# Decode attention: one head's keys for all four batches in one DMA of 16 KB runs, with the scores reading them by stride

## Chip, cores, metric

The kernel runs on one core of one Trainium2 chip. The metric is the device time of one execution in microseconds. "Fast" is the undisturbed state of the chip.

## The reference, cut to what matters

```python
# x: (4 batches, 1 token, D=512). Attention A and gated unit B, applied twice: A B A B
W = 2048                                   # last W keys of a cache of 8192
q = (layernorm(x) @ wq)                    # 32 query heads of 128, 8 key heads, 4 query heads per key head
k = k_cache[:, :, Sk - W:, :]              # (4, 8, 2048, 128) bf16, the same in both attention layers
scores = einsum(q, k) * 128 ** -0.5
x = x + softmax(scores) @ v @ wo           # then x = x + GLU(layernorm(x))
```

For one token per batch there is little arithmetic and much to read: K is 16.8 MB, V as much per layer, weights the rest.

## The kernel before

One Python program makes a list of operations, a list scheduler orders them for each engine with a table of estimated durations, and semaphores are assigned. SBUF holds an arena of 49 slots; a slot is 128 partitions x 4 KB and takes one 512 KB transfer. Loads are issued in one fixed order from the sync queue, and a load waits until its slot is free. K stays in SBUF from layer one to layer two (32 slots); V is loaded twice, except for two tiles that are kept.

A unit of work is one key head with its four batches:

```python
def kv_d(cache, b, h):                       # 512 KB: partition p holds keys 16p..16p+15, a run of 4 KB
    return cache[b, h, SK - W:SK, :].rearrange("(p j) d -> p (j d)", p=128)

# layer one only: transpose K in place on VectorE, 32x32 blocks of 4-byte words (two bf16 each)
v32 = slot_ap(s).bitcast(F32)
P.op("vector", "T%d_%d" % (h, b), ..., lambda v, v32=v32: v.transpose(v32, v32), ...)

# scores: 4 chunks of the contraction x 4 batches; the four batches go to four column groups of PE
for cp in range(4):
    for gi, (h, b) in enumerate(pairs):
        kt = slot_ap(ks[gi]).rearrange("p (j c k t) -> p c t j k", c=2, k=32, t=2)
        pe.matmul(ps[32 * gi:32 * gi + NR, bank, :], qbd[:, q0:q0 + NR],
                  kt[:, cp // 2, cp % 2, :, :], start=(cp == 0), stop=(cp == 3))
```

`t` is the half of a 4-byte word, so neighbouring columns of the moving operand `kt` lie 4 bytes apart. After the scores come maximum, exponential, a matmul and a transpose that turn P (`pt`), the PV matmuls (64 per unit, 16 for each V tile), and the wo matmuls. The order on PE is: scores of unit u+2, then PV of unit u.

Of the kernel before, what the change touches and what calls it, by code (L numbers as in the profile page):

```python
# [6 lines left out]
F32 = mybir.dt.float32  # L7
# [239 lines left out]
class _SlotPool:  # L247
# [13 lines left out]
_TM = dict(  # L261
    sem_lat=100.0, pick_tol=60.0,
    dma_issue=60.0, dma_lat0=900.0, dma_lat1=1100.0, dma_max_out=16,
    bw_4k=412.0, bw_3k=409.0, bw_1k=356.0,
    pe_pair=38.0, pe_small=230.0, pe_f32=450.0, pe_row=80.0, pe_sq=300.0,
    dve_fix=150.0, dve_f32=1.04, dve_small=90.0,
    act_fix=180.0, act_el=0.833,
# [3 lines left out]
def build(nc, A_x, A_k, A_v, A_wq, A_wo, B_wg, B_wu, B_wd, out, cfg=None):  # L271
# [20 lines left out]
    SLOT = NJ * 128  # L292
# [19 lines left out]
    with es:  # L312
# [35 lines left out]

        P = _Plan()
        pool = _SlotPool(NS)  # L350
        SB = (0, 1)
        PB = 2
        OBS = (3, 4)
# [23 lines left out]
        loads = []  # L377
        where = {}

        def take_load():  # L380
            name, emit = loads.pop(0)
            s = pool.alloc()
            where[name] = s
            emit(s)

        def fill():
            while loads and pool.free:
                take_load()

        def need(name):  # L390
            while name not in where:
# [2 lines left out]

        def done(name):
            pool.release(where.pop(name))

        def load_kv(name, cache, b, h):
            loads.append((name, lambda s: dma(str(name), slot_ap(s), kv_d(cache, b, h), w=[("slot", s)])))
# [222 lines left out]
            return [[(h, b) for h in range(u * nh, (u + 1) * nh) for b in g] for u in range(HKV // nh)]  # L622

        def k_transpose(pairs):
            for (h, b) in pairs:
                s = need(("K", h, b))
                v32 = slot_ap(s).bitcast(F32)
                P.op("vector", "T%d_%d" % (h, b), c_dve(1024), lambda v, v32=v32: v.transpose(v32, v32),  # L628
                     r=[("slot", s)], w=[("slot", s)])

        ucount = [0]

        def softmax_unit(tag, pairs):
            u = ucount[0]
            ucount[0] += 1
            k2 = u % 2
            bank = SB[k2]
            ob = OBS[k2]
            ks = [where[("K", h, b)] for (h, b) in pairs]

            def e_s(pe):
                last = None
                for cp in range(4):
                    for gi, (h, b) in enumerate(pairs):
                        kt = slot_ap(ks[gi]).rearrange("p (j c k t) -> p c t j k", c=2, k=32, t=2)
                        q0 = ((b * HKV + h) * 4 + cp) * NR
                        last = pe.matmul(ps[32 * gi:32 * gi + NR, bank, :], qbd[:, q0:q0 + NR],  # L647
                                         kt[:, cp // 2, cp % 2, :, :], start=(cp == 0), stop=(cp == 3))
                return last
            P.op("tensor", "S" + tag, 16 * tm["pe_row"], e_s,  # L650
                 r=[("slot", s) for s in ks] + [("q", i, a) for i in set(h // 4 for (h, b) in pairs) for a in range(4)],
                 w=[("pss", k2)], banks=(bank,))
            mk = mxt[:, k2 * 32:(k2 + 1) * 32]
            P.op("vector", "mx" + tag, c_dve(512),
                 lambda v: v.tensor_reduce(nmax[:, k2:k2 + 1], ps[:, bank, :], AXX, ALU.max),  # L655
                 r=[("pss", k2)], w=[("mx", k2)], banks=(bank,))
            P.op("vector", "mk" + tag, tm["dve_small"],
                 lambda v: v.tensor_scalar(mk, maskr[:, :], nmax[:, k2:k2 + 1], None, ALU.add),
                 r=[("mx", k2), ("maskr",)], w=[("mk", k2)])
            P.op("vector", "nm" + tag, tm["dve_small"],  # L660
                 lambda v: v.tensor_reduce(nmax[:, 2 + k2:3 + k2], mk, AXX, ALU.max, negate=True, apply_transpose=True),  # L661
                 r=[("mk", k2)], w=[("nm", k2)])
            P.op("scalar", "ex" + tag, c_act(512) + 200.0,
                 lambda a: a.activation(prow[:, :], ps[:, bank, :], ACTF.Exp, bias=nmax[:, 2 + k2:3 + k2], scale=1.0,  # L664
                                        accum_out=psm[:, k2:k2 + 1]),
                 r=[("pss", k2)] + [("nm", k2)], w=[("prow",), ("psm", k2)], banks=(bank,))
            return k2

        def turn_p(tag, k2):
            ob = OBS[k2]  # L670
            P.op("tensor", "pp" + tag, tm["pe_sq"],
                 lambda pe: pe.matmul(ps[:, PB, :], perm[:, :], prow[:, :], start=True, stop=True),  # L672
                 r=[("prow",), ("perm",)], w=[("ppb",)], banks=(PB,))
            P.op("vector", "pt" + tag, c_dve(512),
                 lambda v: v.transpose(ebuf[:, k2 * 512:(k2 + 1) * 512], ps[:, PB, :]),  # L675
                 r=[("ppb",)], w=[("e", k2)], banks=(PB,))
            hi, mid, lo = (s3[:, k2 * 3 + n:k2 * 3 + n + 1] for n in range(3))
            sp, sr = psm[:, k2:k2 + 1], sres[:, k2:k2 + 1]
            P.op("gpsimd", "s1" + tag, 200.0, lambda g: g.tensor_copy(hi, sp), r=[("psm", k2)], w=[("s3", k2, 0)])  # L679
            P.op("gpsimd", "s2" + tag, 200.0, lambda g: g.tensor_tensor(sr, sp, hi, ALU.subtract),  # L680
                 r=[("psm", k2), ("s3", k2, 0)], w=[("sr", k2)])
            P.op("gpsimd", "s3" + tag, 200.0, lambda g: g.tensor_copy(mid, sr), r=[("sr", k2)], w=[("s3", k2, 1)])
            P.op("gpsimd", "s4" + tag, 200.0, lambda g: g.tensor_tensor(lo, sr, mid, ALU.subtract),
                 r=[("sr", k2), ("s3", k2, 1)], w=[("s3", k2, 2)])

            def e_sb(pe):
                last = None
                for n, sn in enumerate((hi, mid, lo)):
                    last = pe.matmul(ps[:, ob, 128:128 + NR], sn.broadcast_to([128, 128]), sel_b[:, :],  # L689
                                     start=(n == 0), stop=(n == 2))  # L690
                return last
            P.op("tensor", "sb" + tag, 3 * tm["pe_pair"], e_sb,
                 r=[("s3", k2, n) for n in range(3)] + [("sel_b",)], w=[("psb", k2)], banks=(ob,))
            rv = rinv[:, k2 * NR:(k2 + 1) * NR]
            P.op("vector", "ri" + tag, c_dve(NR) + 60.0,
                 lambda v: v.reciprocal(rv, ps[:, ob, 128:128 + NR]),
                 r=[("psb", k2)], w=[("rinv", k2)], banks=(ob,))
# [50 lines left out]
        def attn(L, gi_, wb):  # L748
            g = GROUPS[gi_]
            us = units_of(g)  # L750
            if L == 2:
                us = us[::-1]
            kuse = 2 * gi_ + (0 if L == 0 else 1)

            def front(ui):
                if L == 0:
                    k_transpose(us[ui])
                k2 = softmax_unit("%d.%d.%d" % (L, gi_, ui), us[ui])
                if L == 2:
                    for p in us[ui]:  # L760
                        done(("K",) + p)
                    fill()
                return k2

            ks = {}
            for ui in range(2):
                ks[ui] = front(ui)
                turn_p("%d.%d.%d" % (L, gi_, ui), ks[ui])
            for ui, pairs in enumerate(us):
                tag = "%d.%d.%d" % (L, gi_, ui)  # L770
                if ui + 2 < len(us):
                    ks[ui + 2] = front(ui + 2)
                ov = pv_unit(tag, pairs, ks[ui], keep if L == 0 else ())
                if ui + 2 < len(us):
                    turn_p("%d.%d.%d" % (L, gi_, ui + 2), ks[ui + 2])
                wo_unit(tag, kuse, wb, pairs, ov, ks[ui], ui == 0, ui == len(us) - 1)
            nb = len(g)
            P.op("vector", "xa%d_%d" % (L, gi_), tm["dve_fix"] + 40.0,
                 lambda v: v.tensor_tensor(bview(xT[:, 0:NX], g[0], g[-1] + 1),
                                           ps[:, wb, 0:NC * nb].rearrange("p (c b) -> p c b", b=nb),  # L780
                                           bview(xT[:, 0:NX], g[0], g[-1] + 1), ALU.add),
                 r=[("psw", wb)] + [("xT", b) for b in g], w=[("xT", b) for b in g], banks=(wb,))
# [66 lines left out]
        add_weights("wq", 0)  # L849
        for gi, g in enumerate(GROUPS):  # L850
            us = units_of(g)
            for (h, b) in us[0] + us[1]:
                load_kv(("K", h, b), A_k, b, h)
            for ui, pairs in enumerate(us):
                if ui + 2 < len(us):
                    for (h, b) in us[ui + 2]:
                        load_kv(("K", h, b), A_k, b, h)
                hs = set(h for h, b in pairs)
                add_weights("wo", 2 * gi, [("wo", h) for h in hs])
                for (h, b) in pairs:  # L860
                    load_kv(("V", h, b), A_v, b, h)
# [104 lines left out]
```

## Time and profile before

| | |
|---|---|
| time, median | 193.9 us |
| span of the profiled run | 191.3 us |
| bytes read | 72.9 MB |
| PE / VectorE busy | 53% / 46% |

In the profiles PE is TensorE (the matmuls), DVE is VectorE, ACT is ScalarE; `L647` is line 647 of the kernel. These are lines of the page of the kernel before: the span, the busy tenths in 40 slices of PE and DMA, the granted PE clock in tenths, and what the DMA engines moved in each slice of 4.8 us.

```profile
span 191.3 us, 4412 instructions
PE   0443224564617264171654436454885999985643
PEclk9999999999999999999999999999995555555555
DMA  4999999999999999999999999999999999999990
GB/s 123 342 413 412 409 409 389 410 393 404 408 392 411 388 406 410 390 411 392 398 398 388 406 407 359 388 380 413 409 409 405 411 406 407 407 407 406 403 366 17
```

The DMA row is full from the third slice to the last but one, near 410 GB/s. The dips to about 390 recur once per unit (about every 11.7 us), as the wo transfers (runs of 1 KB) do, and the dip around slice 25 is the first GLU, where loads wait for slots. So the kernel runs at the pace of the stream. But PE is at 9 tenths in slices 32 to 35: in layer two there is not much room behind the stream.

These are one layer-two unit on PE and the last matmuls that wait for the stream, from the timeline of the kernel before (start, duration, engine and line, how many; in brackets the idle time before and what ended it). A 0.25 us group (L689) is left out.

```profile
153.74 1.88 PE L647 MATMUL ps<-arena,qbd 128*16 128x512 bf16 x16
155.65 0.57 PE L739 MATMUL ps<-onb,arena 128*128 128x4 bf16 x16
156.08 1.85 PE L709 MATMUL ps<-ebuf,arena 128*128 128x4 bf16 x64
157.82 0.61 PE L672 MATMUL ps<-prow,perm 128*128 128x512 bf16 x1
158.36 1.88 PE L647 MATMUL ps<-arena,qbd 128*16 128x512 bf16 x16
...
187.07 1.01 PE L831 MATMUL ps<-hT,arena 128*128 128x4 bf16 x24 [0.63 <-DMA arena<-in_B_w_down_dram]
```

A unit's scores (L647) come 4.62 us apart (158.36 - 153.74). The four V tiles of a unit take 4 x 1.28 = 5.1 us to arrive. So PE has 0.5 us of room per unit. The last w_down lands at 187.07 us, and only 4.2 us of span come after it.

These two lines are the groups of the K transposes and of the score matmuls (busy us, mean ns of one, idle before).

```profile
L628 DVE STREAM_TRANSPOSE arena<-arena 128x1024 f32<-128x1024 f32 x32 | 38.2, 1217 | 0.7 <-DMA arena<-in_A_k_cache_dram 0.3
L647 PE MATMUL ps<-arena,qbd 128*16 128x512 bf16 x256 | 28.4, 587 | 31.2 <-DVE arena L628 31.2
```

The mean of 587 ns is not what a score matmul costs, because four run side by side: 16 take 1.9 us in most units. There is a second speed: at 139 to 141 us, 16 take only 1.1 us (shown with the experiments). "Slower" and "faster speed" below mean these two measured durations. The recorded granted clock does not tell them apart: it was 1.00 in the window 25 to 33 us with the slower speed (1.88 us) and 0.95 in the window 136 to 145 us that holds the faster. In the busiest stretch, 149 to 165 us (PE busy 15.6 of 16 us), it was 0.50 and the scores took 1.88 us. What sets the two speeds stays open here.

### The profile page before, as it was taken

Reading aid. Unit: us, or ns where it says so; the run is one execution under the profiler, and the core shown is the slowest. Engines: PE = TensorE matmul, PEld = TensorE weight load, DVE = VectorE, ACT = ScalarE, POOL = GpSimd, SP = SyncE. Lnnn points to the kernel's source line nnn. Section 1 sums busy time; section 2 is a strip of 40 time slices with the busy share of each in tenths; the row PEclk is TensorE's granted clock in tenths of the full one; section 3 lists DMA queues with packets and bytes.
Section 4 is the critical chain, followed back from the end, with each engine's and each line's share of the span. In section 5 each row is a group of like instructions: output and inputs, shape, how many; then the busy total and the mean of one; then the engine's idle time right before and its main releaser. Section 6 shows DMA issues by size and latency. Waiting matters only on the chain.

```text
span 191.3 us, 4412 instructions
## 1 busy us (share of the span) xinstructions
PE 101.8 (53%) x1920; PEld 57.7 (30%) x1920; DVE 88.8 (46%) x196; ACT 18.8 (10%) x51; POOL 15.2 (8%) x73
## 2 busy tenths in 40 slices
PE   0443224564617264171654436454885999985643
PEld 0110001241404123041244331321245565574222
DVE  6135999295582954729410032123592444421331
ACT  2010000110101001010000000001141111100100
POOL 6000001110101001010010000000032011110000
PEclk9999999999999999999999999999995555555555
DMA  4999999999999999999999999999999999999990
GB/s 123 342 413 412 409 409 389 410 393 404 408 392 411 388 406 410 390 411 392 398 398 388 406 407 359 388 380 413 409 409 405 411 406 407 407 407 406 403 366 17
DMA packets 23556, 73.18 MB, mean 383 GB/s; under 512 B 2280, under 2 KB 6384, under 8 KB 23536
## 3 DMA queue, kind: packets, MB, share of 16 engines
q1 hardware_dynamic: 23536, 72.89, 97.9%
q8 instruction: 15, 0.25, 0.5%
q14 instruction: 5, 0.04, 0.1%
HBM read 72.88 MB, written 0.00 MB: 381 GB/s over the span
## 4 chain that ended last, share of the span: by engine, by line
DMA 40%; SPq 33%; PE 18%; issue 4%; DVE 3%
SPq L369 33%; DMA arena<-in_A_v_cache_dram 12%; DMA arena<-in_B_w_down_dram 11%; DMA arena<-in_A_k_cache_dram 7%; PE ps L709 7%; PE ps L647 6%; DMA arena<-in_B_w_up_dram 5%; DMA arena<-in_A_wq_dram 5%; PE ps L672 1%; PE ps L739 1%; DVE nmax L655 1%; PE ps L831 1%; DVE arena L628 1%; DVE ebuf L675 1%; PE ps L577 1%
## 5 line engine op out<-in xcount | busy, mean ns | idle before, releaser
L647 PE MATMUL ps<-arena,qbd 128*16 128x512 bf16 x256 | 28.4, 587 | 31.2 <-DVE arena L628 31.2
L709 PE MATMUL ps<-ebuf,arena 128*128 128x4 bf16 x1024 | 34.1, 167 | 17.9 <-DMA arena<-in_A_v_cache_dram 14.0
L709 PEld LDWEIGHTS ps<-ebuf,arena 128*128 128x128 bf16 x1024 | 31.4, 104 | 26.2 <-DMA arena<-in_A_v_cache_dram 19.6
L628 DVE STREAM_TRANSPOSE arena<-arena 128x1024 f32<-128x1024 f32 x32 | 38.2, 1217 | 0.7 <-DMA arena<-in_A_k_cache_dram 0.3
L721 DVE TENSOR_TENSOR onb<-ps,rinv 128x16 bf16<-128x16 f32 x16 | 3.1, 195 | 41.0 <-PE ps L709 41.0
L655 DVE TENSOR_REDUCE nmax<-ps 128x1 f32<-128x512 f32 x16 | 10.9, 684 | 21.3 <-PE ps L647 21.1
L664 ACT ACTIVATE prow<-ps,nmax 128x512 bf16<-128x512 f32 x16 | 11.0, 687 | 95.6 <-DVE nmax L661 89.9
L647 PEld LDWEIGHTS ps<-arena,qbd 128*16 128x16 bf16 x256 | 6.5, 109 | 44.2 <-DVE arena L628 27.4
L679 POOL CAST s<-psm 128x1 bf16<-128x1 f32 x16 | 3.0, 189 | 148.6 <-ACT prow L664 148.6
L577 PE MATMUL ps<-arena,xn 128*4 128x512 bf16 x64 | 9.4, 592 | 9.6 <-DMA arena<-in_A_wq_dram 6.7
L675 DVE STREAM_TRANSPOSE ebuf<-ps 128x512 f32<-128x512 f32 x16 | 11.3, 707 | 1.6 <-PE ps L672 1.6
L672 PE MATMUL ps<-prow,perm 128*128 128x512 bf16 x16 | 9.0, 563 | 4.2 <-ACT prow L664 4.1
L739 PE MATMUL ps<-onb,arena 128*128 128x4 bf16 x256 | 9.1, 166 | 3.5 <-issue 2.1
L797 PE MATMUL ps<-arena,xn 128*4 128x448 bf16 x64 | 7.2, 558 | 5.5 <-DVE xn L558 2.9
L739 PEld LDWEIGHTS ps<-onb,arena 128*128 128x128 bf16 x256 | 8.1, 104 | 3.8 <-issue 3.5
L586 DVE STREAM_TRANSPOSE ebuf<-ps 128x512 f32<-128x512 f32 x4 | 2.9, 714 | 9.7 <-PE ps L577 9.7
L831 PE MATMUL ps<-hT,arena 128*128 128x4 bf16 x112 | 4.2, 167 | 4.7 <-DMA arena<-in_B_w_down_dram 3.4
L577 PEld LDWEIGHTS ps<-arena,xn 128*4 128x4 bf16 x64 | 1.5, 83 | 15.8 <-DMA arena<-in_A_wq_dram 12.5
L804 DVE STREAM_TRANSPOSE ebuf<-ps 128x448 f32<-128x448 f32 x4 | 2.6, 650 | 6.9 <-PE ps L797 6.9
L831 PEld LDWEIGHTS ps<-hT,arena 128*128 128x128 bf16 x112 | 3.6, 105 | 6.0 <-DMA arena<-in_B_w_down_dram 5.9
L547 ACT ACTIVATE lnv<-lnv 128x4 f32<-128x4 f32 x4 | 0.8, 206 | 42.2 <-DVE lnv L544 42.2
L689 PE MATMUL ps<-sel_b,s 128*128 128x16 bf16 x48 | 3.7, 177 | 2.3 <-DVE onb L721 1.9
(54 smaller groups left out, 60.1 us busy)
## 6 DMA issues: line engine op xcount, KB each, us to landing
arena<-in_A_v_cache_dram SPq DMA_DIRECT2D x62, 512.0 KB, 12.6
arena<-in_A_k_cache_dram SPq DMA_DIRECT2D x32, 512.0 KB, 13.1
arena<-in_A_wq_dram SPq DMA_DIRECT2D x16, 512.0 KB, 8.0
arena<-in_A_wo_dram SPq DMA_DIRECT2D x8, 512.0 KB, 14.8
arena<-in_B_w_gate_dram SPq DMA_DIRECT2D x8, 448.0 KB, 13.7
arena<-in_B_w_up_dram SPq DMA_DIRECT2D x8, 448.0 KB, 13.2
arena<-in_B_w_down_dram SPq DMA_DIRECT2D x6, 512.0 KB, 9.9
arena<-in_B_w_down_dram SPq DMA_DIRECT2D x2, 256.0 KB, 10.1
```

The costliest lines, as they stand in the source:

```text
L369: o = P.op("sync", name, 0.0, lambda e, dst=dst, src=src: e.dma_start(dst, src), r=r, w=w, dma_bytes=nbytes, dma_rate=tm[rate])
L577: last = pe.matmul(ps[32 * hh:32 * hh + NB, qb, :], xn[:, c * NB:(c + 1) * NB], slot_ap(s)[:, hh * 512:(hh + 1) * 512], start=(c == 0), st ...
L628: P.op("vector", "T%d_%d" % (h, b), c_dve(1024), lambda v, v32=v32: v.transpose(v32, v32), r=[("slot", s)], w=[("slot", s)])
L647: last = pe.matmul(ps[32 * gi:32 * gi + NR, bank, :], qbd[:, q0:q0 + NR], kt[:, cp // 2, cp % 2, :, :], start=(cp == 0), stop=(cp == 3))
L655: lambda v: v.tensor_reduce(nmax[:, k2:k2 + 1], ps[:, bank, :], AXX, ALU.max),
L664: lambda a: a.activation(prow[:, :], ps[:, bank, :], ACTF.Exp, bias=nmax[:, 2 + k2:3 + k2], scale=1.0, accum_out=psm[:, k2:k2 + 1]),
L672: lambda pe: pe.matmul(ps[:, PB, :], perm[:, :], prow[:, :], start=True, stop=True),
L675: lambda v: v.transpose(ebuf[:, k2 * 512:(k2 + 1) * 512], ps[:, PB, :]),
L709: last = pe.matmul(ps[:, ob, gi * REP:(gi + 1) * REP], src[:, j * 128:(j + 1) * 128], ev[:, 1, j, gi * REP:(gi + 1) * REP], start=(j == 0) ...
L739: last = pe.matmul(ps[:, wb, c * nb:(c + 1) * nb], slot_ap(s)[:, r_ * D + c * 128:r_ * D + (c + 1) * 128], ov[:, o0:o0 + nb], start=(first ...
L797: last = pe.matmul(ps[32 * g:32 * g + NB, SB[n], 0:NF], xn[:, c * NB:(c + 1) * NB], slot_ap(s)[:, g * NF:(g + 1) * NF], start=(c == 0), st ...
L831: last = pe.matmul(ps[:, CB, 128 + c * nb:128 + (c + 1) * nb], src[:, (fc - a) * D + c * 128:(fc - a) * D + (c + 1) * 128], hT[:, fc * nb: ...
```

## The change

Its intent: longer runs are read faster (estimated in the prediction as 427 GB/s against 410). 32 K transfers with 4 KB runs become 8 with 16 KB runs. With a dimension of 32 outermost in the source, the batches are interleaved over the partitions: partition 4p+b holds keys 64p to 64p+63 of batch b. The in-place transpose then leaves the four batches interleaved word by word, so the columns of one batch lie 4 words = 16 bytes apart, and the score matmul reads them with that stride. The P transpose undoes the new order of keys with a strided PSUM read. K gets 32 fixed slots, and 17 are left for all other loads.

```diff
+            src = A_k[:, h, SK - W:SK, :].rearrange("b (p j) d -> p b (j d)", p=32)
+            dma("K%d" % h, k4_ap(h), src, w=[("slot", 4 * h + i) for i in range(4)], rate="bw_16k")
...
         pool = _SlotPool(NS)
+        pool.free = list(range(4 * HKV, NS))
...
+            ktv = k4_ap(hk).rearrange("p (j c x y t) -> p c t y j x", c=2, x=8, y=4, t=2)
...
-                        kt = slot_ap(ks[gi]).rearrange("p (j c k t) -> p c t j k", c=2, k=32, t=2)
-                                         kt[:, cp // 2, cp % 2, :, :], start=(cp == 0), stop=(cp == 3))
+                                         ktv[:, cp // 2, cp % 2, b, :, :], start=(cp == 0), stop=(cp == 3))
...
-                 lambda v: v.transpose(ebuf[:, k2 * 512:(k2 + 1) * 512], ps[:, PB, :]),
+                 lambda v: v.transpose(
+                     ebuf[:, k2 * 512:(k2 + 1) * 512],
+                     ps[:, PB, :].rearrange("p (y j x) -> p j x y", y=4, x=8)),
```

More of the change, by code (lines that the diff above doesn't have):

```diff
@@ L263 @@
     dma_issue=60.0, dma_lat0=900.0, dma_lat1=1100.0, dma_max_out=16,
-    bw_4k=412.0, bw_3k=409.0, bw_1k=356.0,
+    bw_16k=428.0, bw_4k=412.0, bw_3k=409.0, bw_1k=356.0,
     pe_pair=38.0, pe_small=230.0, pe_f32=450.0, pe_row=80.0, pe_sq=300.0,
@@ L378, in build, with take_k @@
         where = {}
+        def take_k():
+            while loads and loads[0][0][0] == "K":
+                loads.pop(0)[1](None)
         def take_load():
+            take_k()
             name, emit = loads.pop(0)
@@ L386, in fill @@
         def fill():
+            take_k()
             while loads and pool.free:
                 take_load()
+                take_k()
         def need(name):
@@ L396, in done, with k4_ap, load_k @@
             pool.release(where.pop(name))
+        def k4_ap(h):
+            return arena[:, 4 * h * SLOT:4 * (h + 1) * SLOT]
+        def load_k(h):
+            where[("K", h)] = h
+            src = A_k[:, h, SK - W:SK, :].rearrange("b (p j) d -> p b (j d)", p=32)
+            dma("K%d" % h, k4_ap(h), src, w=[("slot", 4 * h + i) for i in range(4)], rate="bw_16k")
         def load_kv(name, cache, b, h):
@@ L624, in k_transpose @@
         def k_transpose(pairs):
-            for (h, b) in pairs:
-                s = need(("K", h, b))
-                v32 = slot_ap(s).bitcast(F32)
-                P.op("vector", "T%d_%d" % (h, b), c_dve(1024), lambda v, v32=v32: v.transpose(v32, v32),
-                     r=[("slot", s)], w=[("slot", s)])
+            h = pairs[0][0]
+            need(("K", h))
+            for t in range(4):
+                v32 = slot_ap(4 * h + t).bitcast(F32)
+                P.op("vector", "T%d_%d" % (h, t), c_dve(1024), lambda v, v32=v32: v.transpose(v32, v32),
+                     r=[("slot", 4 * h + t)], w=[("slot", 4 * h + t)])
         ucount = [0]
@@ L638, in softmax_unit @@
             ob = OBS[k2]
-            ks = [where[("K", h, b)] for (h, b) in pairs]
+            hk = pairs[0][0]
+            ktv = k4_ap(hk).rearrange("p (j c x y t) -> p c t y j x", c=2, x=8, y=4, t=2)
             def e_s(pe):
@@ L644, in e_s @@
                     for gi, (h, b) in enumerate(pairs):
-                        kt = slot_ap(ks[gi]).rearrange("p (j c k t) -> p c t j k", c=2, k=32, t=2)
                         q0 = ((b * HKV + h) * 4 + cp) * NR
                         last = pe.matmul(ps[32 * gi:32 * gi + NR, bank, :], qbd[:, q0:q0 + NR],
-                                         kt[:, cp // 2, cp % 2, :, :], start=(cp == 0), stop=(cp == 3))
+                                         ktv[:, cp // 2, cp % 2, b, :, :], start=(cp == 0), stop=(cp == 3))
                 return last
             P.op("tensor", "S" + tag, 16 * tm["pe_row"], e_s,
-                 r=[("slot", s) for s in ks] + [("q", i, a) for i in set(h // 4 for (h, b) in pairs) for a in range(4)],
+                 r=[("slot", 4 * hk + t) for t in range(4)] + [("q", i, a) for i in set(h // 4 for (h, b) in pairs) for a in range(4)],
                  w=[("pss", k2)], banks=(bank,))
@@ L759, in front @@
                 if L == 2:
-                    for p in us[ui]:
-                        done(("K",) + p)
+                    for t in range(4):
+                        pool.release(4 * us[ui][0][0] + t)
                     fill()
@@ L851, in build @@
             us = units_of(g)
-            for (h, b) in us[0] + us[1]:
-                load_kv(("K", h, b), A_k, b, h)
+            for u in us[0:2]:
+                loads.append((("K", u[0][0]), lambda _, h=u[0][0]: load_k(h)))
             for ui, pairs in enumerate(us):
                 if ui + 2 < len(us):
-                    for (h, b) in us[ui + 2]:
-                        load_kv(("K", h, b), A_k, b, h)
+                    loads.append((("K", us[ui + 2][0][0]), lambda _, h=us[ui + 2][0][0]: load_k(h)))
                 hs = set(h for h, b in pairs)
```

## The prediction

> **What bounds it now.** The DMA stream. In the page's 40 slices the DMA row is at 9 tenths almost throughout, at 388 to 413 GB/s, with a dip at the first GLU. 72.9 MB at about 407 GB/s is 179 us of the 191.3 us span; the rest is lead-in and a tail of 4 us after the last w_down lands at 187 us (chain of waits). PE is busy 53%, DVE 46%. In the timeline of layer one, PV waits for V tiles that land every 1.28 us (512 KB, 410 GB/s); in layer two PE takes 4.6 us per unit against 5.1 us of V transfer.
>
> **What changes.**
> 1. 32 K transfers of 4 KB runs become 8 of 16 KB runs; bytes stay 16.8 MB. In layer one a unit moves eight 4 KB-run transfers and one wo transfer of 1 KB runs in 11.72 us (one block of K transposes to the next, timeline). Eight at 1.28 us leave 1.48 us for wo. Per engine that is 46 ns per 1 KB run and 160 ns per 4 KB run: 8 ns fixed plus 0.037 ns/byte. Estimate for a 16 KB run: 615 ns, 427 GB/s; 4.92 us per head against 5.12: 0.2 us x 8 = 1.6 us saved, all on the critical path.
> 2. K gets 32 fixed slots, everything else 17 instead of up to 49. Non-K takes 5 slots per 11.7 us, so 17 cover 39 us, against 12.6 us issue-to-landing. Cost about 0.
> 3. Transposes: same count and shape (1217 ns), already back to back and ahead of V. The P transpose now reads PSUM strided: the GLU transpose, strided already, takes 650 ns for 448 columns against 707 for 512 contiguous, the same per column. Cost 0.
> 4. Score matmuls read K with a step of 16 bytes instead of 4. Now 16 take about 1.85 us[...]. [...] No trace here shows this case. I expect little loss[...]. If all doubled (+1.8 us per unit), layer two would become PE bound: +6 to +10 us.
>
> **DMA risk.** The partition is now 4p+b. [...] Each 10% lost on K costs about 4 us.
>
> **Prediction.** 193.98 - 1.6 = about 192.4 us. Range 190.4 to 198.5. Faster by over 2%: 0.08; within 2%: 0.68; slower: 0.24.
>
> **What would show it.** Packets: 4096 of 4 KB become 1024 of 16 KB. The GB/s row in layer one rises by 4 to 8. K transpose blocks come 11.5 us apart, not 11.7. Score matmuls in layer two stay at 1.7 to 1.9 us per unit. The last w_down lands 1.6 us earlier, with the same tail.
>
> **What would make it wrong.** K DMA slower than 410 GB/s[...]: low GB/s in the K slices. 16 KB runs cut into 4 KB packets: no gain. Score matmuls doubled: PE at 9 tenths through layer two, V landed early, a longer tail. A new slot wait of the sync queue in layer one: bubbles in the DMA row.

The forecast's sum came to 193.98 - 1.6 (the K transfers, step 1) = 192.4 us; the other steps stand in it as 0. Cut, where marked, are passages on the hardware that no trace or run shows: in step 4 what tied speeds to the clock, a rule for strided reads, and a term of 0.7 us that the prediction took to be absorbed; under the DMA risk and in the last paragraph, reasons why K might come slower. The cuts take nothing out of the sum but that 0.7 us, which entered it as 0. In the expectations further down, words that tie speeds to the clock are cut too, and once the same rule.

## The result, and the profile after

| | before | after |
|---|---|---|
| time, median | 193.92 us | 205.12 us |
| ratio of fast runs | | 1.0576 (95%: 1.0522 to 1.0631) |

A ratio is the mean time of one kernel's fast runs over that of the other's in the same rounds, so it is not quite the ratio of the medians.

The same lines of the page for the changed kernel (slices of 5.1 us):

```profile
span 203.1 us, 4368 instructions
PE   0451066583744729457288444569998899999663
PEclk9999999967675757558557555557996698866558
DMA  4999999999999999999989999999999999998000
GB/s 134 354 436 429 429 391 415 417 391 443 372 435 387 428 398 407 423 388 392 393 342 339 355 304 368 416 412 412 407 411 401 412 408 407 405 403 330 12 0 4
```

Two things stand out. The K transfers are faster: 429 to 443 GB/s in slices that held 410 before. And the stream ends in slice 37, at about 187 us (36 slices are 182.8 us, and 330 GB/s is four fifths of a slice), where it ended before too. What grew is what comes after it: about 16 us against 4.

The same part of layer two in the changed kernel's timeline, and the GLU at the end (L664 was L647, L816 and L850 are the GLU; again the 0.23 us group, here L708, is left out):

```profile
171.82 3.85 PE L664 MATMUL ps<-arena,qbd 128*16 128x512 bf16 x16
175.69 0.54 PE L758 MATMUL ps<-onb,arena 128*128 128x4 bf16 x16
176.09 1.75 PE L728 MATMUL ps<-ebuf,arena 128*128 128x4 bf16 x64
177.86 0.61 PE L689 MATMUL ps<-prow,perm 128*128 128x512 bf16 x1
178.40 3.84 PE L664 MATMUL ps<-arena,qbd 128*16 128x512 bf16 x16
...
194.30 3.16 PE L816 MATMUL ps<-arena,xn 128*4 128x448 bf16 x32 [1.43 <-DVE xn L574]
198.61 1.54 PE L850 MATMUL ps<-hT,arena 128*128 128x4 bf16 x56 [1.16 <-DVE hT L840]
```

Sixteen score matmuls take 3.85 us where they took 1.88; nothing else in the unit is longer. Units now come 6.58 us apart (178.40 - 171.82), more than the 5.1 us of V. Layer two has become bound by PE. When it is over, all weights have long landed: the GLU waits for its own inputs (xn, hT) and no longer for the DMA.

The same two groups:

```profile
L664 PE MATMUL ps<-arena,qbd 128*16 128x512 bf16 x256 | 61.5, 1082 | 30.3 <-DVE arena L645 30.3
L645 DVE STREAM_TRANSPOSE arena<-arena 128x1024 f32<-128x1024 f32 x32 | 37.1, 1205 | 1.7 <-DMA arena<-in_A_k_cache_dram 1.7
```

The transposes did not change; the score matmuls' busy time more than doubled.

In layer one the timeline of the changed kernel shows a loop (L645 the K transposes, L692 the P transpose):

```profile
71.60 4.56 DVE L645 STREAM_TRANSPOSE arena<-arena 128x1024 f32<-128x1024 f32 x4
76.21 3.85 PE L664 MATMUL ps<-arena,qbd 128*16 128x512 bf16 x16 [4.01 <-DVE arena L645]
80.12 0.69 DVE L672 TENSOR_REDUCE nmax<-ps 128x1 f32<-128x512 f32 x1 [3.96 <-PE ps L664]
81.42 0.69 ACT L681 ACTIVATE prow<-ps,nmax 128x512 bf16<-128x512 f32 x1 [11.37 <-DVE onb L740]
82.26 0.61 PE L689 MATMUL ps<-prow,perm 128*128 128x512 bf16 x1 [0.16 <-ACT prow L681]
82.90 0.72 DVE L692 STREAM_TRANSPOSE ebuf<-ps 128x512 f32<-128x512 f32 x1 [1.50 <-PE ps L689]
83.76 3.43 DVE L645 STREAM_TRANSPOSE arena<-arena 128x1024 f32<-128x1024 f32 x3
```

In VectorE's schedule the next head's transposes stand behind the P transpose of this one, and in the trace they start at 83.76 us, after it (82.90 + 0.72 us). The loop takes 12.16 us (83.76 - 71.60). The stream needs about 11.5 us per unit (4.9 for K, 5.1 for V, 1.5 for wo). So layer one is no longer quite bound by the stream either.

### The profile page after: what moved, and what is told of

Same layout as the page of the kernel before. It is cut to its first block, busy times and chain, and to the rows that moved or that the text cites. A ratio compares the mean times of both kernels' runs of the same rounds, so it can differ in the third digit from the quotient of the medians.

```text
span 203.1 us, 4368 instructions
## 1 busy us (share of the span) xinstructions
PE 129.1 (64%) x1920; PEld 55.8 (27%) x1920; DVE 88.8 (44%) x196; ACT 18.8 (9%) x51; POOL 15.1 (7%) x73
## 2 busy tenths in 40 slices
DMA packets 20100, 73.18 MB, mean 360 GB/s; under 512 B 1896, under 2 KB 6000, under 8 KB 19056
## 3 DMA queue, kind: packets, MB, share of 16 engines
q1 hardware_dynamic: 20080, 72.89, 91.6%
## 4 chain that ended last, share of the span: by engine, by line
PE 48%; DVE 24%; DMA 15%; issue 4%; ACT 3%; SPq 3%; POOL 2%; ACTq 0%
PE ps L664 30%; DVE arena L645 15%; PE ps L728 8%; DMA arena<-in_A_k_cache_dram 7%; DMA arena<-in_A_wq_dram 4%; DMA arena<-in_B_w_down_dram 4%; SPq L370 3%; DVE nmax L672 3%; PE ps L758 2%; ACT prow L681 2%; PE ps L689 2%; PE ps L816 2%; PE ps L708 1%; PE ps L850 1%; DVE ebuf L692 1%
## 5 line engine op out<-in xcount | busy, mean ns | idle before, releaser
L664 PE MATMUL ps<-arena,qbd 128*16 128x512 bf16 x256 | 61.5, 1082 | 30.3 <-DVE arena L645 30.3
L645 DVE STREAM_TRANSPOSE arena<-arena 128x1024 f32<-128x1024 f32 x32 | 37.1, 1205 | 1.7 <-DMA arena<-in_A_k_cache_dram 1.7
L728 PEld LDWEIGHTS ps<-ebuf,arena 128*128 128x128 bf16 x1024 | 28.6, 100 | 13.3 <-issue 13.2
L728 PE MATMUL ps<-ebuf,arena 128*128 128x4 bf16 x1024 | 30.1, 165 | 3.1 <-issue 1.8
L664 PEld LDWEIGHTS ps<-arena,qbd 128*16 128x16 bf16 x256 | 7.1, 101 | 60.1 <-issue 35.0
L692 DVE STREAM_TRANSPOSE ebuf<-ps 128x512 f32<-128x512 f32 x16 | 11.4, 713 | 10.8 <-PE ps L689 10.8
L689 PE MATMUL ps<-prow,perm 128*128 128x512 bf16 x16 | 7.7, 482 | 3.2 <-ACT prow L681 3.1
L816 PE MATMUL ps<-arena,xn 128*4 128x448 bf16 x64 | 6.7, 568 | 4.4 <-DVE xn L574 2.9
L850 PE MATMUL ps<-hT,arena 128*128 128x4 bf16 x112 | 3.7, 166 | 4.9 <-DMA arena<-in_B_w_down_dram 3.7
L708 PEld LDWEIGHTS ps<-sel_b,s 128*128 128x128 bf16 x48 | 2.3, 100 | 14.4 <-issue 9.1
L708 PE MATMUL ps<-sel_b,s 128*128 128x16 bf16 x48 | 3.6, 174 | 3.4 <-POOL s L702 3.3
L715 DVE RECIPROCAL rinv<-ps 128x16 f32<-128x16 f32 x16 | 3.8, 244 | 3.4 <-PE ps L708 3.4
L850 PEld LDWEIGHTS ps<-hT,arena 128*128 128x128 bf16 x112 | 3.3, 100 | 6.4 <-DMA arena<-in_B_w_down_dram 4.3
```

Source lines behind the costliest of these rows:

```text
L645: P.op("vector", "T%d_%d" % (h, t), c_dve(1024), lambda v, v32=v32: v.transpose(v32, v32), r=[("slot", 4 * h + t)], w=[("slot", 4 * h + t)])
L664: last = pe.matmul(ps[32 * gi:32 * gi + NR, bank, :], qbd[:, q0:q0 + NR], ktv[:, cp // 2, cp % 2, b, :, :], start=(cp == 0), stop=(cp == 3))
L689: lambda pe: pe.matmul(ps[:, PB, :], perm[:, :], prow[:, :], start=True, stop=True),
L692: lambda v: v.transpose(ebuf[:, k2 * 512:(k2 + 1) * 512], ps[:, PB, :].rearrange("p (y j x) -> p j x y", y=4, x=8)),
L708: last = pe.matmul(ps[:, ob, 128:128 + NR], sn.broadcast_to([128, 128]), sel_b[:, :], start=(n == 0), stop=(n == 2))
L728: last = pe.matmul(ps[:, ob, gi * REP:(gi + 1) * REP], src[:, j * 128:(j + 1) * 128], ev[:, 1, j, gi * REP:(gi + 1) * REP], start=(j == 0) ...
```

## The experiments

Theory A: the 16-byte step of the score read is the whole loss. Rival B: 17 slots for everything but K starve the stream. Rival C: K arriving 2 MB at a time delays the transposes.

All runs below passed the comparison with the reference, also those that read wrong keys. In this problem the scores are so small that the softmax is nearly flat, so the comparison hardly sees them (an estimate from the reference: keys and q both have a spread of about 0.05, which makes scores of about 0.05 x 0.05 = 0.0025). The last experiment makes up for a part of that, for the one version that matters.

### Undo the stride alone

```diff
-  ktv[:, cp // 2, cp % 2, b, :, :]
+  slot_ap(4 * hk + b).rearrange("p (j c k t) -> p c t j k", c=2, k=32, t=2)[:, cp // 2, cp % 2, :, :]
```

> The changed kernel in all respects (16 KB transfers, fixed slots, strided P transpose), but each score matmul reads one 512 KB quarter of its head with the old step of 4 bytes; result wrong on purpose. Theory A (the 16-byte step of the score read is the whole loss): 16 score matmuls take 1.7 to 1.9 us again, and the time is about 192.4 us, that is the before less the 1.6 us of the K transfers. Rival B (17 slots for all but K starve the DMA stream) or rival C (K arriving 2 MB at a time delays the transposes): score matmuls fast, but the time stays above 196 us.

Measured: 192.49 us against 193.18 of before, ratio 0.9945 (0.9911 to 0.9979). Layer-two scores take 1.88 us per 16 again, and this is their group:

```profile
L664 PE MATMUL ps<-arena,qbd 128*16 128x512 bf16 x256 | 27.9, 579 | 11.7 <-DVE arena L645 11.4
```

Everything else of the change is in this kernel, so B and C cannot explain the loss. The saving is 1.1 us by the ratio, less than the 1.6 predicted.

### Put the stride into the kernel before

```diff
-  kt = slot_ap(ks[gi]).rearrange("p (j c k t) -> p c t j k", c=2, k=32, t=2)
+  kt = slot_ap(ks[gi]).rearrange("p (n e) -> p e n", e=8)          # 8 bf16 = 16 bytes
-  kt[:, cp // 2, cp % 2, :, :]
+  kt[:, cp::4, :]
```

> The kernel before, only the score matmuls read their K tile with a step of 16 bytes (two passes of 256 elements, wrong on purpose). Theory A: 16 score matmuls take about 3.85 us as in the changed kernel, and the time is 203 to 207 us. Rivals B and C: score matmuls slower perhaps, but the time within 2 us of before.

Measured: 205.63 us, ratio 1.0642 (1.0619 to 1.0666), and this group in its profile:

```profile
L647 PE MATMUL ps<-arena,qbd 128*16 128x512 bf16 x256 | 60.7, 1079 | 31.4 <-DVE arena L628 31.4
```

The stride alone makes the loss, in a kernel that has none of the rest of the change. Theory A holds from both sides.

### The slot split alone

The kernel before, with K in slots 0 to 31 and `pool.free = list(range(32, 49))` for the rest.

> The kernel before with K in 32 fixed slots and 17 slots for all else, nothing else changed; result right. Theory A: 193.5 to 194.5 us, as before. Rival B: slower by several us, with low GB/s where the sync queue waits for slots.

Measured: 193.45 us against 193.18, ratio 1.0011 (0.9988 to 1.0034). The split costs nothing. Rival B falls.

### How the cost depends on the step

Two single looks (one run each, so their state is unknown; read the matmuls, not the times). The edit is that of the first experiment, with `"p (n e) -> p e n"` and e = 4 (8 bytes) or e = 16 (32 bytes). The 16-byte "line" in the expectations was hypothesis.

> The changed kernel with the score read at a constant step of 8 bytes (wrong on purpose). If time goes with 16-byte lines touched by the four concurrent matmuls, 16 of them take half of 3.85 us, about 1.9 us[...]; total about 192 to 193.5 us. If any step above 4 bytes costs alike, 3.85 us and 204 us.

> The changed kernel with the score read at a step of 32 bytes (wrong on purpose). If the cost is one line fetch of 16 bytes per element, it stays at 3.85 us per 16 matmuls and 205 us, since a wider step touches no more lines. If cost grows with distance, or the line is 32 bytes wide, it rises to about 7 us per 16 and the time is far above 210 us.

From their timelines, 8 bytes first and then 32 bytes:

```profile
138.61 1.99 PE L664 MATMUL ps<-arena,qbd 128*16 128x512 bf16 x16 [0.65 <-ACT prow L681]
```

```profile
140.60 3.84 PE L664 MATMUL ps<-arena,qbd 128*16 128x512 bf16 x16
```

And the kernel before, at about the same place, with its step of 4 bytes:

```profile
138.89 1.12 PE L647 MATMUL ps<-arena,qbd 128*16 128x512 bf16 x16
```

So 16 matmuls take 1.1 us (PE at its faster speed) or 1.9 us (at its slower) with 4 bytes, 2.0 us with 8 bytes at either place, and 3.85 us with 16 or 32 bytes. The times agree: 192.16 us with 8 bytes, 206.53 with 32. Going from 16 to 32 bytes costs the matmuls nothing more (3.85 and 3.84 us), and 8 bytes cost about half (2.0 us). From 8 bytes on the times go with the number of 16-byte stretches that a read touches: one per element at 16 and 32 bytes, one per two elements at 8. With stretches of 32 bytes, 16 would have been cheaper than 32; with stretches of 8, 8 would have cost as much as 16.

Two elements per stretch (8 bytes) cost about what PE takes anyway at its slower speed (2.0 against 1.9 us); at its faster speed they are not free (2.0 against 1.1 us).

### Is it a rate shared by the four concurrent matmuls?

```diff
-  pe.matmul(ps[32 * gi:32 * gi + NR, bank, :], ..., start=(cp == 0), stop=(cp == 3))
+  pe.matmul(ps[0:NR, bank, :], ..., start=(cp == 0 and gi == 0), stop=(cp == 3 and gi == 3))
```

> The changed kernel with its 16-byte step, but the four matmuls of a step all write the same 16 PSUM rows, so they use one column group and run one after the other instead of four at once (wrong on purpose). If the limit is the rate of line fetches shared by the four concurrent streams (0.95 us for 4 x 512 elements, 0.46 ns each), one stream alone is not slowed[...]. If each matmul by itself is slow at this step (0.95 us for 512 elements), 16 take about 15 us and the time is far over 300 us.

> Control for the run with one column group: the same serial score matmuls, but at a step of 4 bytes (wrong on purpose). There each took 0.87 us at 16 bytes. If that was the step, [...]the time falls to 220 to 270 us. If one column group is slow for another reason, about 14 us per 16 again.

(Cut from these two are times of a single stream at two clocks.)

The scores with one column group and a step of 16 bytes, from its timeline, then the control with 4 bytes:

```profile
42.12 13.91 PE L664 MATMUL ps<-arena,qbd 128*16 128x512 bf16 x16 [3.21 <-DVE arena L645]
```

```profile
25.41 6.05 PE L664 MATMUL ps<-arena,qbd 128*16 128x512 bf16 x16 [7.58 <-DVE arena L645]
```

I had thought of a rate shared by four streams. That falls: alone, each matmul takes 0.87 us (13.91 / 16) for 512 columns at 16 bytes, hardly less than a group of four side by side (3.85 / 4 = 0.96 us). Each stream pays by itself, 0.87 us / 512 = 1.7 ns for each column (one 16-byte stretch each), and four streams pay at the same time (0.96 us for the four). The control takes 0.38 us each (6.05 / 16) and in layer two 0.23 us. An estimate from these: 512 columns at 4 bytes touch 128 stretches, 128 x 1.7 ns = 0.22 us, no more than the control took; at 8 bytes 256 stretches make 0.44 us, close to the 0.50 us measured for a group of four. (Both are single looks: 364.31 and 224.36 us.)

### Which layer loses it

The 16-byte read in one layer only, the 4-byte read of the first experiment in the other.

> The changed kernel with its 16-byte score read in the first attention layer only; the second layer reads with 4 bytes (wrong on purpose). The prediction held that layer one has room for slow score matmuls, 0 us; against that, the trace of the changed kernel shows its K transposes 12.2 us apart where DMA needs 11.5, in a loop transposes 4.5, scores 3.9, maximum 0.7, exponential 0.8 and the P turn 1.4: then layer one ends 1 to 3 us later and the time is 193.5 to 196 us.

> The changed kernel with its 16-byte score read in the second attention layer only. If the loss of 11.8 us sits where PE was already close behind the stream of V, this run has nearly all of it: 200 to 204 us. If the two layers share it, 197 to 200 us.

Measured: layer one only 194.42 us, ratio 1.0043 (0.9959 to 1.0126); layer two only 202.61 us, 1.0460 (1.0393 to 1.0527). Against the ratio without any 16-byte read (0.9945), layer one costs about 1.0% or 1.9 us and layer two about 5.2% or 10 us. Together that is 6.2%; the whole change shows 1.0576 / 0.9945, or 6.3%. These ratios are from different rounds, and their intervals are wide: about 1.6 us either way for the run with layer one only, 1.3 us for layer two only, 0.7 us for the run without. So layer two's 10 us is clear, but layer one's 1.9 us is not clear of noise by the times alone (0.9959 to 1.0126 overlaps 0.9911 to 0.9979). The traces support it: the last wo matmuls of layer one start at 112.12 us in the changed kernel, against 110.12 us with the stride undone.

### A correct version with a short step, first try

The transposes can write each row of a 32x32 block in another order. Batch-major order puts the eight columns of one batch side by side:

```diff
-  v.transpose(v32, v32)
+  v.transpose(v32.rearrange("p (j y x) -> p j x y", y=4, x=8), v32)      # write step 32 bytes
-  ktv = ....rearrange("p (j c x y t) -> p c t y j x", c=2, x=8, y=4, t=2)
+  ktv = ....rearrange("p (j c y x t) -> p c t y j x", c=2, x=8, y=4, t=2)  # read step 4 bytes
```

> The changed kernel, but the K transposes write their 32x32 blocks batch-major, so that the 8 columns of one batch are neighbours and the score read has a step of 4 bytes; result right. Theory A: score matmuls back to 1.7 to 1.9 us per 16 and, if the strided write costs the transposes nothing (1.2 us each), 192.0 to 193.0 us, a little better than before. If the strided write makes the transposes twice as long (2.4 us), layer one is bound by them and the time is over 200 us.

```profile
L645 DVE STREAM_TRANSPOSE arena<-arena 128x1024 f32<-128x1024 f32 x32 | 59.5, 1961 | 1.4 <-DMA arena<-in_A_k_cache_dram 1.4
L665 PE MATMUL ps<-arena,qbd 128*16 128x512 bf16 x256 | 28.3, 588 | 50.7 <-DVE arena L645 42.1
```

Measured: 200.60 us, ratio 1.0402 (1.0368 to 1.0437). The scores are back at their old speed, but a transpose that writes with a step of 32 bytes takes 1961 ns instead of 1217. The cost has moved to VectorE, and layer one's loop is longer still (transposes start at 62.20 and 75.22 us, 13.0 us apart). Whether this in-place write leaves the right keys on the chip was not tested.

### A correct version, second try: pairs

Meet in the middle. Write pairs of columns of one batch, so that the write step is 8 bytes and the read has two elements per 16 bytes:

```diff
-  v.transpose(v32, v32)
+  v.transpose(v32.rearrange("p (j y z) -> p j z y", y=4, z=2), v32)
-  ktv = ....rearrange("p (j c x y t) -> p c t y j x", c=2, x=8, y=4, t=2)
+  ktv = ....rearrange("p (j c w y z t) -> p c t y j w z", c=2, w=4, y=4, z=2, t=2)
```

> The changed kernel; the K transposes write each 32-column row of a block as groups of two neighbours of one batch (write step 8 bytes), so the score read takes pairs 4 bytes apart and then jumps 32 bytes: two elements per 16-byte line. Result right. If [...]an 8-byte write step costs the transposes nothing: 16 score matmuls 1.7 to 2.0 us, transposes 1.2 us, time 192.0 to 193.0 us. If the loss goes with the number of 16-byte lines touched, counted for four matmuls at once (3.85 us for one element per line), two per line cost about 1.9 us[...]. If writes also slow down with 8 bytes, transposes at 1.5 us or more and a time over 195 us.

These are its two groups, and a row of its page:

```profile
L645 DVE STREAM_TRANSPOSE arena<-arena 128x1024 f32<-128x1024 f32 x32 | 37.5, 1217 | 6.3 <-DMA arena<-in_A_k_cache_dram 6.2
L665 PE MATMUL ps<-arena,qbd 128*16 128x512 bf16 x256 | 32.4, 635 | 13.4 <-DVE arena L645 11.3 <-ACT prow L682 1.1 <-issue 0.8
```

```profile
GB/s 125 342 426 441 434 421 373 432 384 423 407 392 443 374 423 410 396 444 375 392 401 390 407 395 332 375 387 413 411 410 405 407 407 406 412 403 404 404 351 14
```

Measured: 191.66 us against 193.86, ratio 0.9892 (0.9860 to 0.9924). The transposes cost what they did, 16 scores take 2.0 us, and the kernel is 1.1% faster than before: the best version, though by less than 2%. The read has the step of neither earlier test: pairs 4 bytes apart, then a jump. It still takes the 2.0 us of the constant 8-byte step, which also has two elements per 16 bytes. So in these runs the time follows the count of elements per 16 bytes, not the width of the jump.

### Is that version right on the chip?

The pair version was changed to check itself: heads 0 and 5 are loaded again, transposed out of place in plain order, and a million times the summed squared difference is added to x.

> A test of data, not of time. The comparison with the reference may be blind to the scores, since runs that read wrong K on purpose passed it. So the pair-writing kernel here loads heads 0 and 5 a second time, transposes them out of place in plain order, subtracts the in-place pair-ordered result, and adds a million times the sum of the squared differences to the residual stream. If the in-place write with its permuted order is right on the chip, the difference is 0 and the result stays correct; if any element differs by the size of the keys, the result is far off and counted wrong. The time is of no interest (extra loads and work, 46 slots): 215 to 260 us.

Measured: correct (263.74 us, longer than I guessed, of no interest). The in-place transposes with the permuted write left the right keys in these two heads. Off the chip I tried the same test with the order wrong, and it made x explode. The test does not cover the score read or the order of P: that these then meet the right keys follows from the index arithmetic of the access patterns, and no run on the chip tests it.

## Why the prediction was wrong

The predicted 192.4 us was 12.7 us below the 205.1 measured. Going through its steps:

- **The stream bounds the kernel: right.**
- **1, the K transfers gain 1.6 us: right in size.** In the window 17 to 27 us, which holds only K, the stream ran at 429 GB/s in the changed kernel and 410 before. The first two heads' transposes, which wait for K, start 4.90 us apart (20.49 and 25.39 us), against 4.92 estimated. And where nothing else was slow, the last V tile of layer one was used earlier by the expected amount: at 110.57 us before, at 109.16 with the stride undone and at 108.91 in the pair version, so 1.4 and 1.7 us. The packets came as predicted too (1024 of over 8 KB on the queue: 20080 less 19056), but the changed kernel's transposes came 12.16 us apart and not 11.5. How much reaches the end is less certain: 1.1 us with the stride undone, 2.1 in the pair version, with intervals that just overlap (0.9911 to 0.9924). Part can be given back at the first GLU, where the loads wait for slots (323 GB/s from 115 to 120 us with the stride undone, 355 before). I did not test that.
- **2, the slots cost nothing: right** (ratio 1.0011).
- **3, the transposes cost nothing more: right** (1205 ns, and 713 ns for the P transpose against 707, with its strided PSUM read).
- **4, "I expect little loss": wrong, and this is the step that failed.** The read with one element per 16 bytes takes 0.96 us per four matmuls whether PE is at its slower or faster speed, against 0.47 us expected at the slower speed (1.88 / 4). That PE was at its faster speed and the read no quicker shows in two neighbouring lines of the changed kernel: the P turn takes 0.39 us here (0.61 at the slower speed), the scores 3.85.

```profile
143.41 0.39 PE L689 MATMUL ps<-prow,perm 128*128 128x512 bf16 x1
143.72 3.85 PE L664 MATMUL ps<-arena,qbd 128*16 128x512 bf16 x16
```

That little would be lost was the author's estimate; no run before the change had shown such a read. An estimate from the runs: with one element per 16 bytes a column takes 1.7 ns (`onecol`), and with the 4-byte step PE at its slower speed takes a column every 0.9 ns (0.47 us / 512).
- **The size of the alternative was also short.** The prediction named "if all doubled" as a possibility with +6 to +10 us. It counted only layer two. All did double, and layer two alone cost about 10 us; layer one added about 1.9 (not clear of noise by the times, but seen in the traces) through the loop of transposes, scores and softmax (12.16 us in the trace, against the 11.5 us of the stream), which the prediction took to have room ("already back to back and ahead of V").
- **The DMA risk did not come true.** Packets of 16 KB interleaved over the partitions ran at 429 GB/s.

The signs that the prediction gave for this failure are all in the profile: PE at 9 tenths in layer two, a stream that is done early, and a longer tail.

## What to carry to other kernels

Moving a layout's cost from the DMA to a strided engine read is not free because the bytes are the same: count how many elements the read takes from each 16 bytes (here one took 3.85 us per 16 matmuls, two 2.0), and measure one matmul with that step before relying on it. When a layout must interleave, look for the order in which the writer's step and the reader's step are both short; here 8 bytes on the write and pairs on the read cost almost nothing, while 32 bytes on the write or 16 on the read cost 61% (1961 against 1217 ns) and 105% (3.85 against 1.88 us). And an engine 0.5 us per unit behind the bottleneck is part of the bottleneck: doubling its dearest step turned a predicted gain of 1.6 us into a loss of 11.
